# Recurrent-memory attention: output projection of the last tokens for four blocks at once, and a PSUM bank of its own for the memory's softmax sums

One core of a Trainium2 chip runs the kernel. The metric is device time in microseconds (us). Before the change it took 2135.5 us (median of 4 runs from 2131.47 to 2164.58).

## The reference, cut to what matters

```python
def _A_ref(x, mem0, Wq, Wk, Wv, Wo, seg_len):   # x: 1 x 2048 x 512, 32 heads of 128, seg_len 32, mem: 8 x 512
    mem = mem0
    for s in range(n_seg):                       # 64 segments, one after another
        h = concatenate([mem, xs])               # 8 memory rows + 32 tokens
        q, k, v = ...                            # h times Wq, Wk, Wv
        p = softmax(where(mask, q k^T * scale, -1e9))
        o = einsum('bhte,hed->btd', p v, Wo)
        mem = o[:, :M]                           # the next segment needs these 8 rows
        outs.append(o[:, M:])
x = x + A(layernorm(x));  x = x + B(layernorm(x))     # B is a gMLP block
x = x + A(layernorm(x));  x = x + B(layernorm(x))
```

Only the 8 memory rows of o must go around the loop. The last 8 tokens of a segment (rows 24 to 31) are handled separately: the kernel collects their attention outputs in a tile `oB` and multiplies them by Wo later. This deferred product is called "y pass" here. A block is 128 tokens, that is four segments; j4 is a segment's place in its block.

## The kernel before

The end of a segment. `fill()` issues a piece of independent TensorE work. psO takes four PSUM banks, and columns 320 to 383 of each hold sums of the memory rows:

```python
psO = attO.tile([P, 4, 512], F32, name="psO")
psD = att.tile([P, 2, 512], F32, name="psD")
for r in range(2):
    for g in range(2):
        o = psO[:, 2 * r + g, 320:384]
        sums(r, g, o, o, 0, 8, True)       # ones (64 rows) times E: the memory rows' softmax sums
pv(0)                                       # products of the first half of the heads, into psO
...                                         # sums of the tokens, into psD
pv(1)                                       # second half, into psO
Rm = segp.tile([P, 4, 64], F32, name="Rm")
inverse(Rm[:], psO[:, :, 320:384])          # 1/sum as Exp(-Ln(sum)), ScalarE
Rt = segp.tile([P, 2, 512], F32, name="Rt")
inverse(Rt[:], psD[:])
nc.vector.tensor_tensor(out=hview(uT_cur, 0, 4, 0, 8), in0=oview(0, 4, 0, 8), in1=Rm[:]..., op=ALU.mult)
fill(); fill(); run(copies); tok_out(0)
pw = acc.tile([P, 512], F32, name="pw")
wo_pass(pw, uT_cur)                         # memory rows times Wo: the recurrence
build_hA(s + 1, pw)                         # masked copy and transpose: the next segment's input
store_o(s, pw)
fill(); fill(); run(copies); tok_out(1); run(turns)
spare()                                     # layer norm of later blocks, y_add
```

The y pass of one block, in the fills of j4 = 0 of the next one, and the end of the A block:

```python
def wo_pass(po, lhs, heads=range(H)):
    for h in heads:
        n = ...
        for cg in range(4):                 # four quarter-array matmuls of 128 columns
            nc.tensor.matmul(po[32 * cg:32 * cg + 32, 0:128], lhsT=lhs[:, n, :], rhs=wo_rhs(h, cg), ...,
                             tile_position=(0, 32 * cg))
def y_pass(tb):
    pwB = acc.tile([P, DM], F32, name="pwB")
    for h0 in range(0, H, 8):
        wo_pass(pwB, blk_state[tb]["oB"], range(h0, h0 + 8))
        if h0 + 8 < H: yield
    ...                                     # ScalarE copies pwB, 64 KB go to oB_d in memory
def y_load(tb): ...                         # x, oA_d (tokens 0-23) and oB_d (24-31) into xs_y and ot_y, one buffer each
def y_add(tb): ...                          # ot_y + xs_y, store to xd, statistics for the next layer norm

# after the 64 segments:
for _ in y_pass(NB - 1): pass
for tb in (NB - 2, NB - 1):                 # only two blocks are left
    y_load(tb); y_add(tb)
```

The softmax here doesn't subtract the row's maximum and nothing guards it: scores larger than these inputs give would overflow.

## Time and profile before

The two A blocks are recurrences, so I split the profiled execution at the starts of the matmul group pw, the product that gives the next memory, and at the last aggregate of layer-norm statistics, which releases the B block. "Last pw" is that of the 64th segment; one more pw, for the tokens of that segment, follows it and counts as part of the end. All values are us.

| part of the profiled run | before |
|---|---|
| start to first pw of A1 | 88.0 |
| A1, first to last pw (63 intervals) | 789.8 |
| A1, last pw to last aggregate | 20.0 |
| B1, to the first pw of A2 | 247.6 |
| A2, first to last pw | 784.7 |
| A2, last pw to last aggregate | 20.8 |
| B2 to the end | 177.4 |
| span | 2128.3 |

In the list of waits of the whole run (engine, tile and line, then the releaser; us in total, times, longest) the kernel before has

```profile
ACT Rm L619 <- PE psO L614: 211.4, 128, 2.4
DVE uT L671 <- ACT Rm L620: 178.1, 128, 2.7
```

Such totals say who waits for whom and not what that costs: ScalarE's 211 us are mostly time in which it has nothing else to do. What counts is the wait that reaches TensorE, in the group of pw (count | busy us, mean ns | idle us before it and the main releaser):

```profile
L488 PE MATMUL pw<-Wo_sb,uT 128*32 128x128 bf16 x16640 | 267.6, 220 | 81.8 <-DVE uT L671 61.5
```

### The profile page before, as it was taken

To read this page: it belongs to the slowest core of one execution; us is meant where nothing else is said; L and a number is where in the kernel's file an instruction comes from. 1 tells how busy PE (TensorE), PEld (TensorE's weight loads), DVE (VectorE), ACT (ScalarE), POOL (GpSimd) and SP (SyncE) were. 2 spreads that over 40 slices of the span, in tenths; PEclk is the share of its full clock that TensorE was granted. 3 is DMA by queue.
4 is the path that set the end of the run, shared out by engine and by line. 5 is a ranking of instruction groups with operands and counts; after the bars stand their busy time and mean duration, and the time that the engine had idled before them with its cause. 6 is when DMAs were issued, how large, how long until landed. Compare 5 with 4: busy or idle time off the path is not lost.

```text
span 2128.3 us, 104406 instructions
## 1 busy us (share of the span) xinstructions
PE 1811.6 (85%) x48640; PEld 1108.3 (52%) x48640; DVE 1211.8 (57%) x2577; ACT 1031.6 (48%) x1828; POOL 138.8 (7%) x287
## 2 busy tenths in 40 slices
PE   0599999999998999583987999999999999986899
PEld 0355555555555555442754555555555555554476
DVE  1566666666666666440334666666666666664322
ACT  0455555555555555370004555655555555554500
POOL 2000000000000000001230000000000000000022
PEclk9999999999999999895998999999999999997999
DMA  9201111111111110327651011111111111104253
GB/s 382 88 25 35 37 35 35 35 36 38 41 38 35 38 43 27 120 62 267 154 164 61 26 35 35 35 43 36 38 37 46 38 38 37 31 25 155 50 139 90
DMA packets 178675, 145.33 MB, mean 68 GB/s; under 512 B 97472, under 2 KB 148288, under 8 KB 175168
## 3 DMA queue, kind: packets, MB, share of 16 engines
q1 hardware_dynamic: 152544, 83.76, 14.4%
q10 hardware_dynamic: 21728, 30.78, 4.1%
q0 software_dynamic: 3968, 24.12, 3.1%
q8 instruction: 380, 6.23, 1.2%
q14 instruction: 55, 0.45, 0.1%
HBM read 88.13 MB, written 33.70 MB: 57 GB/s over the span
## 4 chain that ended last, share of the span: by engine, by line
PE 65%; ACT 14%; DVE 8%; issue 6%; DMA 6%; POOL 0%; SPq 0%; ACTq 0%; POOLq 0%; DVEq 0%
PE psm L397 21%; PE pw L488 9%; PE pg L216 8%; PE psv L397 6%; PE psb L397 5%; DVE KA L565 4%; PE psO L614 4%; ACT rows L561 4%; PE psS L585 3%; ACT Rm L620 3%; DMA wspT<-in_B_w_sp_dram 2%; ACT Rm L619 2%; DVE uT L671 2%; PE psO L604 2%; PE pwB L488 2%
## 5 line engine op out<-in xcount | busy, mean ns | idle before, releaser
L397 PEld LDWEIGHTS <-hA 128*32 128x32 bf16 x12288 | 305.9, 96 | 300.4 <-DVE hA L537 33.5
L561 ACT CAST rows<-psm 128x512 bf16<-128x512 f32 x512 | 299.7, 585 | 176.6 <-PE psm L397 176.6
L488 PE MATMUL pw<-Wo_sb,uT 128*32 128x128 bf16 x16640 | 267.6, 220 | 81.8 <-DVE uT L671 61.5
L488 PEld LDWEIGHTS <-uT 128*32 128x32 bf16 x16640 | 238.1, 97 | 139.6 <-DVE uT L671 112.2
L397 PE MATMUL psm<-Wq_sb,hA 128*32 128x512 bf16 x4096 | 277.0, 380 | 15.3 <-issue 9.3
L397 PE MATMUL psm<-Wk_sb,hA 128*32 128x512 bf16 x4096 | 271.8, 379 | 0.0
L397 PE MATMUL psv<-Wv_sb,hA 128*32 128x512 bf16 x4096 | 268.0, 382 | 0.0
L630 DVE TENSOR_TENSOR uT<-psO,Rt 128x384 bf16<-128x384 f32 x256 | 137.9, 539 | 201.9 <-ACT Rt L620 201.9
L565 DVE STREAM_TRANSPOSE QQ<-rows 128x512 bf16<-128x512 bf16 x256 | 181.9, 711 | 82.0 <-ACT rows L561 81.8
L216 PE MATMUL pg<-wspT,z2n 128*128 128x256 bf16 (+1 forms) x1536 | 177.0, 277 | 55.1 <-DMA wspT<-in_B_w_sp_dram 55.1
L565 DVE STREAM_TRANSPOSE KA<-rows 128x512 bf16<-128x512 bf16 x256 | 181.8, 710 | 38.2 <-ACT rows L561 35.7
L216 PEld LDWEIGHTS <-z2n 128*128 128x128 bf16 (+1 forms) x1536 | 151.3, 100 | 80.6 <-issue 62.6
L590 ACT ACTIVATE E<-psS 128x448 bf16<-128x448 f32 x256 | 140.0, 547 | 107.5 <-PE psS L585 107.5
L571 DVE CAST VA<-psv 128x512 bf16<-128x512 f32 x256 | 175.4, 685 | 2.4
L397 PEld LDWEIGHTS <-hB 128*32 128x32 bf16 x3072 | 78.3, 97 | 159.9 <-DVE hB L446 71.5
L219 DVE TENSOR_TENSOR gb<-pg,bsp_bc 128x256 f32<-128x256 f32 x96 | 40.6, 423 | 207.5 <-PE pg L216 207.5
L671 DVE TENSOR_TENSOR uT<-psO,Rm 128x256 bf16<-128x256 f32 x128 | 54.3, 424 | 178.1 <-ACT Rm L620 178.1
L619 ACT ACTIVATE Rm<-psO 128x256 f32<-128x256 f32 x128 | 49.0, 383 | 211.4 <-PE psO L614 211.4
L397 PE MATMUL psb<-Wq_sb,hB 128*32 128x512 bf16 x1024 | 70.0, 395 | 91.0 <-DVE hB L446 71.5
L530 POOL COPY QQ<-QTB 128x256 bf16<-128x256 bf16 x128 | 49.4, 401 | 1496.0 <-DVE QTB L476 960.3
L585 PEld LDWEIGHTS <-KA 128*64 128x64 bf16 x2048 | 79.8, 113 | 127.8 <-DVE KA L565 126.5
L620 ACT ACTIVATE Rt<-Rt 128x1024 f32<-128x1024 f32 x128 | 135.4, 1058 | 4.1
(93 smaller groups left out, 2525.3 us busy)
## 6 DMA issues: line engine op xcount, KB each, us to landing
xs<-xd SPq DMA_DIRECT2D x48, 256.0 KB
xs<-xd ACTq DMA_DIRECT2D x48, 256.0 KB
oA_d<-o_sb SPq DMA_DIRECT2D x130, 64.0 KB
xs_y<-xd SPq DMA_DIRECT2D x32, 256.0 KB
xd<-ot_y SPq DMA_DIRECT2D x32, 256.0 KB
Wq_sb<-in_A_Wq_dram POOLq DMA_DIRECT2D x6, 1024.0 KB, 16.0
Wk_sb<-in_A_Wk_dram POOLq DMA_DIRECT2D x6, 1024.0 KB, 24.3
Wv_sb<-in_A_Wv_dram POOLq DMA_DIRECT2D x6, 1024.0 KB, 20.5
```

Source lines behind the costliest of these rows:

```text
L216: nc.tensor.matmul(pg[0:fsz, :], lhsT=z2n[:, st_i, f0:f0 + fsz], rhs=wspT[:, st_i, :], start=(st_i == 0), stop=(st_i == NT - 1))
L397: nc.tensor.matmul(ps[32 * cg:32 * cg + 32, :], lhsT=lhs(kt, cg), rhs=rhs(kt, cg), start=(kt == 0), stop=(kt == KT - 1), tile_position=(0, ...
L488: nc.tensor.matmul(po[32 * cg:32 * cg + 32, 0:128], lhsT=lhs[:, n, :], rhs=wo_rhs(h, cg), start=(h == 0), stop=(h == H - 1), tile_position ...
L561: nc.scalar.copy(r[:], ps[:])
L565: nc.vector.transpose(out=QQ[:, j % 2, :, 0:32] if j < 2 else KA[:, j % 2], in_=r[:])
L571: nc.vector.tensor_copy(VA[:, r].rearrange("p i e -> p (i e)"), ps)
L585: nc.tensor.matmul(pS[64 * g:64 * g + 64, i, c0:80 if K is KA else 112], lhsT=K[:, r, n:n + 2, :].rearrange("p h k -> p (h k)"), rhs=q if ...
L590: nc.scalar.activation(out=E[r][:], in_=pS, func=ACT.Exp, scale=scale)
L619: nc.scalar.activation(out=o, in_=in_, func=ACT.Ln)
L620: nc.scalar.activation(out=o, in_=o, func=ACT.Exp, scale=-1.0)
L630: nc.vector.tensor_tensor(out=hview(uT_nxt, 2 * r, 2 * r + 2, 8, 32), in0=oview(2 * r, 2 * r + 2, 8, 32), in1=Rr[:, :, :, 0:24], op=ALU.mult)
L671: nc.vector.tensor_tensor(out=hview(uT_cur, 0, 4, 0, 8), in0=oview(0, 4, 0, 8), in1=Rm[:].rearrange("p b (n q) -> p b n q", q=8), op=ALU.mult)
```

## The change

Its intent: the memory's sums get a bank of their own, so their reciprocal can start while TensorE still fills psO; and the y pass of 16 segments (512 tokens, 128 deferred rows) runs once, on the whole array. Core of the diff:

```diff
+    onesG = cp.tile([P, 2, P], BF16, name="onesG")       # full-array ones, half of the rows zero
-            for r in range(2):
-                for g in range(2):
-                    o = psO[:, 2 * r + g, 320:384]
-                    sums(r, g, o, o, 0, 8, True)
+            psM = acc.tile([P, 512], F32, name="psM")
+            for g in range(2):
+                o = psM[:, 128 * g:128 * g + 128]
+                nc.tensor.matmul(o, lhsT=onesG[:, g, :], rhs=a_part(0, P, 0, 2, 0, 8), start=(g == 0), ...)
+                nc.tensor.matmul(o, lhsT=onesG[:, g, :], rhs=b_part(0, P, 0, 2, 0, 8), start=False, ...)
...
-            inverse(Rm[:], psO[:, :, 320:384])
+            inverse(Rm[:].rearrange("p g r c -> p (g r c)"), psM[:, 0:256])
...                                                        # uT in two multiplies, one per half
+            spare()                                       # moved here, ahead of the fills
             fill(); fill()
...
-            spare()
...
+        def wo_last(G, heads, pwB):                       # one 128x512 matmul a head
+            for h in heads: ...
+                nc.tensor.matmul(pwB[:], lhsT=oBs[G][:, n, :], rhs=Wo_sb[:, h, :]..., ...)
+        def y_part(G, q): ...                             # 8 heads in j4 = 0 of the q-th block of the next group;
+                                                          # VectorE adds the four partial results in yB
...
-                more = y_pass(tb - 1) if tb > 0 else iter(())
+                more = y_part(tb // 4 - 1, tb % 4) if tb > 3 else iter(())
...
-        for _ in y_pass(NB - 1): pass
-        for tb in (NB - 2, NB - 1):
+        for _ in wo_last(NB // 4 - 1, range(H), pwB): pass
+        for tb in due + list(range(NB - 4, NB)):          # 11, then 12 to 15; block 10 is in flight
             y_load(tb); y_add(tb)
...
-    ident_f = cp.tile(...); maskf = cp.tile(...)          # constants needed only to build others
+    ident_f = tmp.tile(...); maskf = tmp.tile(...)        # pool is closed after the constants: memory used again
-        vsp = ctx.enter_context(tc.tile_pool(name="a_vs", bufs=3))
+        vsp = ctx.enter_context(tc.tile_pool(name="a_vs", bufs=2))
```

The last two pieces make room for the larger `oB`.

More of the change, by code (lines that the diff above doesn't have):

```diff
@@ L53, in _consts @@
     cp = ctx.enter_context(tc.tile_pool(name="consts", bufs=1))
+    tctx = ExitStack()
+    tmp = tctx.enter_context(tc.tile_pool(name="consts_tmp", bufs=1))
     c = {}
-    ident_f = cp.tile([P, P], F32, name="ident_f")
+    ident_f = tmp.tile([P, P], F32, name="ident_f")
     nc.gpsimd.memset(ident_f[:], 0.0)
@@ L62, in _consts @@
     nc.vector.memset(eps_t[:], LN_EPS)
-    maskf = cp.tile([P, 4, 112], F32, name="maskf")
+    maskf = tmp.tile([P, 4, 112], F32, name="maskf")
     nc.gpsimd.memset(maskf[:], 0.0)
@@ L86, in _consts @@
     nc.vector.memset(ones[:], 1.0)
+    onesG = cp.tile([P, 2, P], BF16, name="onesG")
+    nc.vector.memset(onesG[:], 0.0)
+    for g in range(2):
+        nc.vector.memset(onesG[64 * g:64 * g + 64, g, :], 1.0)
     maskM = cp.tile([P, P], mybir.dt.uint16, name="maskM")
@@ L91, in _consts @@
     c["maskM"] = maskM
-    c.update(ident_f=ident_f, ident_bf=ident_bf, eps_t=eps_t, maskN=maskN, ones=ones)
     c["MV"] = [cp.tile([P, 16, 2], F32, name=f"MV{i}") for i in range(2)]
+    tctx.close()
+    c.update(ident_bf=ident_bf, eps_t=eps_t, maskN=maskN, ones=ones, onesG=onesG)
     return c
@@ L275 @@
     c["oA_d"] = dram.tile([S // SEG + 1, P, P], F32, name="oA_d")
-    c["oB_d"] = dram.tile([S // P, P, P], F32, name="oB_d")
+    c["oB_d"] = dram.tile([S // 512, P, DM], F32, name="oB_d")
     nblocks = opts["nblocks"]
@@ L356, in a_block @@
     scale = float(DH) ** -0.5
-    maskN, ones = c["maskN"], c["ones"]
+    maskN, ones, onesG = c["maskN"], c["ones"], c["onesG"]
     with ExitStack() as ctx:
@@ L450, in ln_turn @@
             blk_state[tb].update(hB=hB, KTB=KTB, QTB=QTB, VB=VB)
-        copies, turns = [], []
+        copies, turns, adds = [], [], []
         def run(todo):
@@ L489, in wo_pass, with y_part @@
                                      start=(h == 0), stop=(h == H - 1), tile_position=(0, 32 * cg))
-        def y_pass(tb):
+        yB = {}
+        def wo_last(G, heads, pwB):
+            for h in heads:
+                n = h // 8 * 8 + 2 * (h % 4) + h // 4 % 2
+                nc.tensor.matmul(pwB[:], lhsT=oBs[G][:, n, :], rhs=Wo_sb[:, h, :].rearrange("p (kt g el) -> p g kt el", kt=4, g=4),
+                                 start=(h == heads[0]), stop=(h == heads[-1]))
+                if h % 2 == 1:
+                    yield
+        def y_part(G, q):
             pwB = acc.tile([P, DM], F32, name="pwB")
-            for h0 in range(0, H, 8):
-                wo_pass(pwB, blk_state[tb]["oB"], range(h0, h0 + 8))
-                if h0 + 8 < H:
+            for k, _ in enumerate(wo_last(G, range(8 * q, 8 * q + 8), pwB)):
+                if k < 3:
                     yield
             def out():
-                oB_sb = wk.tile([P, P], F32, name="oB_sb")
-                nc.scalar.copy(oB_sb[:], pwB[:, 0:128])
-                nc.sync.dma_start(oB_d[tb], oB_sb[:])
-            copies.append(out)
+                if q == 0:
+                    yB[G] = wk.tile([P, DM], F32, name="yB", bufs=1)
+                    nc.vector.tensor_copy(yB[G][:], pwB[:])
+                else:
+                    nc.vector.tensor_tensor(out=yB[G][:], in0=pwB[:], in1=yB[G][:], op=ALU.add)
+                if q == 3:
+                    nc.sync.dma_start(oB_d[G], yB.pop(G)[:])
+            adds.append(out)
             yield
@@ L513, in y_load @@
                 nc.sync.dma_start(ot[32 * j + 24:32 * j + 32, :, :],
-                                  oB_d[tb].rearrange("(cg r) c -> r cg c", cg=4)[8 * j:8 * j + 8])
+                                  oB_d[tb // 4, 32 * (tb % 4) + 8 * j:32 * (tb % 4) + 8 * j + 8, :].rearrange("r (cg c) -> r cg c", cg=4))
             xo = ot[:].rearrange("p cg c -> p (cg c)")
@@ L524, in a_block @@
         seg_state = {}
+        oBs = {}
         def prep_segment(s):
@@ L551, in segment @@
             uT_cur, uT_nxt = uT[s % 2], uT[(s + 1) % 2]
-            if j4 == 0:
-                blk_state[tb]["oB"] = blkp.tile([P, H, 32], BF16, name="oB")
-            oB = blk_state[tb]["oB"]
-            E = [None] * 2
+            if s % 16 == 0:
+                oBs[tb // 4] = blkp.tile([P, H, P], BF16, name="oB")
+            oB = oBs[tb // 4]
+            E = segp.tile([P, 2, 4, 112], BF16, name="E")
             def qk(j):
@@ L588, in scores, with a_part, b_part @@
                                              start=(i == 0 and K is KA), stop=True, tile_position=(0, 64 * g), skip_group_check=True)
-                E[r] = segp.tile([P, 4, 112], BF16, name="E")
-                nc.scalar.activation(out=E[r][:], in_=pS, func=ACT.Exp, scale=scale)
+                nc.scalar.activation(out=E[:, r], in_=pS, func=ACT.Exp, scale=scale)
             def close(r):
-                nc.vector.tensor_tensor(out=E[r][:], in0=E[r][:], in1=maskN[:, j4, :].unsqueeze(1).to_broadcast([P, 4, 112]), op=ALU.mult)
-            def b_part(r, g, lo, hi):
-                return E[r][64 * g:64 * g + 64, :, 80:112].rearrange("p i (s q) -> p i s q", s=2)[:, :, :, lo:hi]
-            def a_part(r, g, lo, hi):
-                return E[r][64 * g:64 * g + 64, :, 0:80].rearrange("p i (s q) -> p i s q", s=2)[:, :, :, lo:hi]
-            def sums(r, g, o, oB, lo, hi, first):
-                w = ones[64 * g:64 * g + 64, :]
-                nc.tensor.matmul(o, lhsT=w, rhs=a_part(r, g, lo, hi), start=first, stop=True, skip_group_check=True)
-                nc.tensor.matmul(oB, lhsT=w, rhs=b_part(r, g, 0 if lo == 0 else 8, 8 if lo == 0 else 16),
-                                 start=False, stop=True, skip_group_check=True)
+                nc.vector.tensor_tensor(out=E[:, r], in0=E[:, r], in1=maskN[:, j4, :].unsqueeze(1).to_broadcast([P, 4, 112]), op=ALU.mult)
+            def a_part(p0, p1, r0, r1, lo, hi):
+                e = E[p0:p1, r0:r1].rearrange("p r i c -> p (r i) c")[:, :, 0:80]
+                return e.rearrange("p n (s q) -> p n s q", s=2)[:, :, :, lo:hi]
+            def b_part(p0, p1, r0, r1, lo, hi):
+                e = E[p0:p1, r0:r1].rearrange("p r i c -> p (r i) c")[:, :, 80:112]
+                return e.rearrange("p n (s q) -> p n s q", s=2)[:, :, :, lo:hi]
             def pv(r):
@@ L614, in pv @@
                             nc.tensor.matmul(o if V is VA else ends(o), lhsT=V[64 * g:64 * g + 64, r, i, :],
-                                             rhs=E[r][64 * g:64 * g + 64, i, c0:c1].rearrange("p (s q) -> p s q", s=2),
-                                             start=False, stop=True, skip_group_check=True)
+                                             rhs=E[64 * g:64 * g + 64, r, i, c0:c1].rearrange("p (s q) -> p s q", s=2),
+                                             start=(i == 0 and V is VA), stop=True, skip_group_check=True)
             def inverse(o, in_):
@@ L631, in tok_out @@
                                         in1=Rr[:, :, :, 0:24], op=ALU.mult)
-                nc.vector.tensor_tensor(out=hview(oB, 2 * r, 2 * r + 2, 8 * j4, 8 * j4 + 8), in0=oview(2 * r, 2 * r + 2, 32, 40),
+                nc.vector.tensor_tensor(out=hview(oB, 2 * r, 2 * r + 2, 8 * (s % 16), 8 * (s % 16) + 8), in0=oview(2 * r, 2 * r + 2, 32, 40),
                                         in1=Rr[:, :, :, 24:32], op=ALU.mult)
@@ L653, in segment @@
             v_out(1, v1[:])
+            psM = acc.tile([P, 512], F32, name="psM")
+            for g in range(2):
+                o = psM[:, 128 * g:128 * g + 128]
+                nc.tensor.matmul(o, lhsT=onesG[:, g, :], rhs=a_part(0, P, 0, 2, 0, 8), start=(g == 0), stop=True, skip_group_check=True)
+                nc.tensor.matmul(o, lhsT=onesG[:, g, :], rhs=b_part(0, P, 0, 2, 0, 8), start=False, stop=True, skip_group_check=True)
             psO = attO.tile([P, 4, 512], F32, name="psO")
             psD = att.tile([P, 2, 512], F32, name="psD")
-            for r in range(2):
-                for g in range(2):
-                    o = psO[:, 2 * r + g, 320:384]
-                    sums(r, g, o, o, 0, 8, True)
@@ L661, in segment @@
-            pv(0)
-            for r in range(2):
-                for g in range(2):
-                    o = psD[:, g, 256 * r:256 * r + 256]
-                    sums(r, g, o, o.rearrange("p (n q) -> p n q", q=32)[:, :, 24:32], 8, 40, r == 0)
-            pv(1)
-            Rm = segp.tile([P, 4, 64], F32, name="Rm")
-            inverse(Rm[:], psO[:, :, 320:384])
-            Rt = segp.tile([P, 2, 512], F32, name="Rt")
-            inverse(Rt[:], psD[:])
-            nc.vector.tensor_tensor(out=hview(uT_cur, 0, 4, 0, 8), in0=oview(0, 4, 0, 8),
-                                    in1=Rm[:].rearrange("p b (n q) -> p b n q", q=8), op=ALU.mult)
+            pv(0)
@@ new lines, in segment @@
+            for part, q0, q1, c0 in ((a_part, 8, 40, 0), (b_part, 8, 16, 24)):
+                for r in range(2):
+                    for g in range(2):
+                        o = psD[:, g, 256 * r:256 * r + 256].rearrange("p (n q) -> p n q", q=32)[:, :, c0:32]
+                        nc.tensor.matmul(o, lhsT=ones[64 * g:64 * g + 64, :], rhs=part(64 * g, 64 * g + 64, r, r + 1, q0, q1),
+                                         start=(part is a_part and r == 0), stop=True, skip_group_check=True)
@@ new lines, in segment @@
+            pv(1)
+            Rm = segp.tile([P, 2, 2, 64], F32, name="Rm", bufs=1)
+            inverse(Rm[:].rearrange("p g r c -> p (g r c)"), psM[:, 0:256])
+            Rt = segp.tile([P, 2, 512], F32, name="Rt", bufs=1)
+            inverse(Rt[:], psD[:])
+            for r in range(2):
+                nc.vector.tensor_tensor(out=hview(uT_cur, 2 * r, 2 * r + 2, 0, 8), in0=oview(2 * r, 2 * r + 2, 0, 8),
+                                        in1=Rm[:, :, r].rearrange("p g (n q) -> p g n q", q=8), op=ALU.mult)
@@ L684, in segment @@
             run(copies)
+            run(adds)
             tok_out(1)
             run(turns)
-            spare()
             if s + 1 < NSEG:
@@ L700, in a_block @@
         prep_segment(0)
+        due, ys = [], []
         for s in range(NSEG):
@@ L703, in a_block @@
             if j4 == 0:
-                if tb > 1:
-                    y_load(tb - 2)
-                more = y_pass(tb - 1) if tb > 0 else iter(())
+                more = y_part(tb // 4 - 1, tb % 4) if tb > 3 else iter(())
             if j4 == 1:
@@ L712, in spare @@
             def spare():
+                if ys:
+                    y_add(ys.pop(0))
+                if tb % 4 == 3 and j4 == 1 and tb > 4:
+                    due.extend(range(tb - 7, tb - 3))
+                if due:
+                    ys.append(due.pop(0))
+                    y_load(ys[0])
                 if j4 == 0 and tb + 1 < NB:
                     ln_turn(tb + 1)
-                if j4 == 0 and tb > 1:
-                    y_add(tb - 2)
                 if j4 == 3 and tb + 2 < NB:
@@ L723, in a_block @@
         store_o(NSEG, pw)
-        for _ in y_pass(NB - 1):
-            pass
-        run(copies)
-        for tb in (NB - 2, NB - 1):
+        pwB = acc.tile([P, DM], F32, name="pwB")
+        for _ in wo_last(NB // 4 - 1, range(H), pwB):
+            pass
+        yl = wk.tile([P, DM], F32, name="yB", bufs=1)
+        nc.scalar.copy(yl[:], pwB[:])
+        nc.sync.dma_start(oB_d[NB // 4 - 1], yl[:])
+        for tb in ys:
+            y_add(tb)
+        for tb in due + list(range(NB - 4, NB)):
             y_load(tb)
```

## The prediction

> **What bounds the kernel now.** I read the page first, then all waits, then the timeline of some segments (a segment is 32 tokens; each of the two A blocks runs 64 of them in sequence), then the chain of the end of an A block. The page:
>
> ```profile
> PE   1811.6 (85%) x48640; PEld 1108.3 (52%) x48640; DVE 1211.8 (57%) x2577; ACT 1031.6 (48%) x1828; POOL 138.8 (7%) x287
> ...
> PE 65%; ACT 14%; DVE 8%; issue 6%; DMA 6%; POOL 0%; SPq 0%; ACTq 0%; POOLq 0%; DVEq 0%
> ```
>
> TensorE is the busiest, yet a third of the chain is not TensorE: the recurrence hops PE, ACT, DVE and back. The timeline of one ordinary segment shows the hop that the change is about:
>
> ```profile
> 511.23 0.39 DVE L593 TENSOR_TENSOR E<-E,maskN 128x448 bf16<-128x448 bf16 x1 [0.25 <-ACT E L590]
> ...
> 512.62 0.18 PE L614 MATMUL psO<-E,VB 64*128 64x32 bf16 x2
> 512.73 0.55 PEld L397 LDWEIGHTS <-hB 128*32 128x32 bf16 x16
> 512.73 1.05 PE L397 MATMUL psb<-Wq_sb,hB 128*32 128x512 bf16 x16
> 512.84 0.38 ACT L619 ACTIVATE Rm<-psO 128x256 f32<-128x256 f32 x1 [1.65 <-PE psO L614]
> 513.26 0.42 ACT L620 ACTIVATE Rm<-Rm 128x256 f32<-128x256 f32 x1
> 513.58 1.01 ACT L619 ACTIVATE Rt<-psD 128x1024 f32<-128x1024 f32 x1
> 513.71 0.42 DVE L671 TENSOR_TENSOR uT<-psO,Rm 128x256 bf16<-128x256 f32 x1 [1.37 <-ACT Rm L620]
> 514.18 1.79 PEld L488 LDWEIGHTS <-uT 128*32 128x32 bf16 x128 [0.90 <-DVE uT L671]
> 514.18 1.97 PE L488 MATMUL pw<-Wo_sb,uT 128*32 128x128 bf16 x128 [0.41 <-DVE uT L671]
> ```
>
> Rm reads the memory's sums, complete at about 511.9, but starts only after the last product of the second half (512.62 + 0.18), because both sit in the banks of psO. So Ln, Exp and the multiply (512.84 to 514.13) run in the open; the filler psb hides 0.87 of it and PE stands idle 0.41. After pw, masked copy and transpose lead to the next psm at 517.06. With no filler, pw-to-pw is 11.97 us as well (852.34 to 864.31), so the ordinary segment is bound by this chain, and filler is free. From the 128 starts of pw: in all intervals but those around j4 = 0 (the first segment of a block of 128 tokens) 11.97 is the floor. Above 63 x 11.97 = 754 the first A block has 35.7 us, the second 30.6; 25.5 and 26.8 of it lie behind the pw of j4 = 0. There the old y pass sits:
>
> ```profile
> 437.65 1.35 PE L488 MATMUL pw<-Wo_sb,uT 128*32 128x128 bf16 x83 [0.51 <-issue]
> ...
> 441.67 0.46 PE L488 MATMUL pwB<-Wo_sb,oB 128*32 128x128 bf16 x19 [2.05 <-issue]
> ```
>
> 256 tiny matmuls and as many weight loads in a row, then PE stops with nothing to wait for; then psm waits for the copy out of pwB.
>
> The end of an A block is a chain of transfers: block 15 is loaded, added, its statistics taken, and only then can the B block start (rstd needs all 16).
>
> ```profile
> 891.15 2.15 DMA oB_d<-oB_sb
> 893.32 0.27 SPq L513
> ...
> 894.31 1.65 DMA ot_y<-oB_d
> ```
>
> The first and last of these are from the chain of waits, the middle one the queue's issue; in the timeline what follows is:
>
> ```profile
> 896.14 0.69 DVE L520 TENSOR_TENSOR ot_y<-ot_y,xs_y 128x512 f32<-128x512 f32 x1 [13.89 <-DMA ot_y<-oB_d]
> 896.86 0.34 SPq L521 DMA_DIRECT2D xd<-ot_y  x1
> ```
>
> **What the Trainium skill says.** "PSUM — Partial Sum Buffer", section on bank collisions: two engines must be kept apart by bank and 32-partition quadrant, not by address. The trace agrees: Rm waits for matmuls that write other columns of its banks. "TensorE: Matmul & The Clock Gate", Back-to-back issue gap: N/2.4 + 2.5 ns, 216 for 512 columns; here groups of 16 psm matmuls, each on a quarter of the array and four at once, follow one another at 0.87 us (505.95, 506.82, 507.69), 4 x 217 ns, so it agrees. "Runtime: NRT & Kernel Launch", Instruction fetch mechanics: instructions are streamed in 16 KiB blocks of 256. The page's instruction queue has 380 packets and 6.23 MB, 16.4 KB each, and the stops in pw and pwB fall at fixed places in the stream; that they are fetch is my reading, not shown. "DMA: Bandwidth & Descriptors", Anatomy: about 2 us fixed per transfer, mostly the receipt; the 64 KB store above took 2.15, so it agrees.
>
> **The change, part by part.** (1) Sums. Eight matmuls of 64 columns become four of 128 on the full array. They need both halves of E, ready at 511.62. I put four times 56 ns from there plus one switch of array shape, 0.09 (the gap seen between the end of one stream and the next shape), so the first product starts at 511.97 instead of 511.73. The psD sums take 0.27; the second half then starts at 512.49 rather than 512.38, where it waited for VA anyway: 0.11 lost. psM is complete at 512.03; Rm's Ln and Exp run 512.08 to 512.92, uT follows in two pieces of about 0.28 (128x128 pieces of oB take 0.277) to 513.44. Rt follows Rm on ACT and ends at 514.99 instead of 515.68, so the token products that stand ahead of the masked copy on DVE end at 515.69. On PE: last product issued 512.73, filler from 512.84 to 513.71, pw from 513.76 (32 groups of four at 55.6 ns stream in 1.78; with the 0.19 until the last result is in PSUM, 515.73), masked copy 515.78, transpose and psm 0.68 later as before (516.38 to 517.06): 516.46. The second filler ends at the same moment (515.60 + 0.87). Saved: 0.60 with DVE and PE nearly tied, I take 0.58. Without filler the Rt path decides: 0.69.
>
> (2) y. 2048 quarter-array matmuls per A block (16 x 128) become 128 of 512 columns; PE drops from 48640 to 48640 - 4096 - 512 + 256 = 44288 matmuls. Of the time in it only the excess around j4 = 0 counts. What comes in its place: in 12 segments per A block, two times four matmuls of 216. The second four end 516.7 in the frame above, then DVE adds 128x512 f32 (0.69, as in xo) before psm may take that bank: psm at 517.44, so +0.38 each over 11.97, 4.6 per A block. Some fetch stops stay; I keep 6.
>
> (3) y_add, ln_turn and ln_apply move into the gap of DVE between uT and Rt (1.5 us); y_add is 0.65 + 0.69 + 0.18. Nearly free.
>
> Per A block: 45 segments with filler x 0.58 = 26.1; 7 without x 0.69 = 4.8; excess 35.7 (30.6) less 10.6 = 25.1 (20.0). Sum 56 and 51, 107. Ten chained hops never all come as sums say; I take 100.
>
> (4) The end. Before, two blocks are left for after the last segment, and the first is prefetched. After, 10 is in flight, 11 to 15 are left, and xs_y and ot_y have one buffer each, so load, add and store run one after another. A round: eight issues 0.335 apart and 1.65 landing = 4.0, wait 0.2, add 0.7, store about 2.3 (0.34 to issue and the fixed part; stores here made the next load wait up to 2.9) = 7.2. Block 11 goes beside the last Wo pass: 32 x 0.216 = 6.9 us in place of 2.3 plus its stops of 1.2 to 4. Then 12, 13 and 14 are three rounds in the open (21.6), the larger copy and store cost about 0.5, and the rest of the 11 round and slower pass about 4: +26 per A block, +52.
>
> Sum: 2135.6 - 100 + 52 = 2087.6.
>
> **Rivals.** (a) The end costs more: the queue might keep program order, so that block 10's store waits for yB's; one more round each, +15: 2103. Against: the queue already runs out of program order (block 14's load comes before block 15's oB store). Or early loads of the next block's weights slow the stores: one xd store took 8.27 us at 1934.30. (b) The psM switch costs several tenths, or uT's first piece waits for the whole of psO: then PE and DVE, nearly tied, lose 0.2 to 0.3 per segment, 128 x 0.25 = 32: 2120. (c) The stops behind pwB were all due to the flood of small instructions and vanish, and the chain gains all it can: 2075; with a tail that hides two rounds, 2060. (d) Fetch stops move to pw, which alone still sends 256 instructions in 1.8 us and now has less idle ahead of it: half of the 45 us I count for excess comes back: 2110.
>
> **Range and chances.** The gain in the loop is 100 +- 13, the loss at the end 52 +- 12, independent: 48 +- 18, so 2088, 8 in 10 between 2064 and 2112. The 2% mark below 2135.6 is 2092.9, slightly above my middle; the two fast runs before (2131 and 2136) put it at 2091. Faster 0.56, same 0.41, slower 0.03.
>
> **What would show it.** Rm starts before the second half of the products ends, and PE's wait for uT before pw (61.5 us in all) falls below 10. Ordinary pw-to-pw intervals: 11.4. Intervals behind j4 = 0: 12.3 with a y part. PE's stops without a cause inside pwB are gone. From the last pw to the last aggregate of statistics: 20.0 and 20.8 us before, 46 after. ACT copies of pwB vanish; DVE gains 24 adds or copies of 0.69. The prediction is wrong if the ordinary interval stays above 11.7 (step 1), if the end grows by under 15 or over 40 us (step 4), or if the time moves elsewhere, as into the B blocks.

## The result

The kernel after took 2103.01 us (median of 4 runs, 2101.05 to 2104.00; before 2135.51 in the same rounds). The ratio is 0.9858, with a 95% interval of 0.984 to 0.9877: 1.4% faster, which lies within 2%. Ratios here are the mean time of one kernel's runs over that of the other's runs of the same rounds, so not quite the ratio of the medians. Executions over 1.5% slower than the fastest of the same kernel are left out of the means.

| part of the profiled run | before | after | difference | predicted |
|---|---|---|---|---|
| start to first pw of A1 | 88.0 | 92.2 | +4.3 | 0 |
| A1 loop | 789.8 | 736.4 | -53.4 | -56 computed |
| A1 end | 20.0 | 54.2 | +34.2 | +26 |
| B1 to first pw of A2 | 247.6 | 250.8 | +3.2 | 0 |
| A2 loop | 784.7 | 734.8 | -50.0 | -51 computed |
| A2 end | 20.8 | 55.0 | +34.1 | +26 |
| B2 to the end | 177.4 | 178.9 | +1.6 | 0 |
| span | 2128.3 | 2102.3 | -26.0 | -48, with 100 taken for the 107 |

The profiled run before was one of the faster ones, so the profiles differ by 26.0 and the medians by 32.5.

The loop did what was predicted; starts and ends cost more. From the page of the kernel after:

```profile
PE   1788.5 (85%) x44288; PEld 1076.1 (51%) x44288; DVE 1247.1 (59%) x2732; ACT 1024.3 (49%) x1798; POOL 138.6 (7%) x287
...
PE 66%; ACT 11%; DVE 9%; issue 7%; DMA 4%; SPq 1%; POOL 1%; ACTq 0%; DVEq 0%; POOLq 0%
```

4352 matmuls are gone, yet TensorE's busy time hardly moved (1811.6 to 1788.5), because four quarter-array matmuls ran side by side. ScalarE's share of the chain fell from 14% to 11%. The waits and the group that answer to those of before:

```profile
ACT Rm L636 <- PE psM L676: 117.6, 128, 1.1
```

```profile
L495 PE MATMUL pw<-Wo_sb,uT 128*32 128x128 bf16 x16640 | 266.6, 219 | 30.5 <-issue 23.4
```

uT is no longer what pw waits for: of the 30.5 us left, 23.4 are stops without a visible cause. The timeline of a segment that has a y part (columns: start, length, engine, line, operation, tiles; idle before and releaser in brackets):

```profile
512.11 0.22 PE L676 MATMUL psM<-E,onesG 128*128 128x128 bf16 x1
...
512.37 0.38 ACT L636 ACTIVATE Rm<-psM 128x256 f32<-128x256 f32 x1 [0.92 <-PE psM L676]
...
512.52 0.44 PE L684 MATMUL psD<-E,ones 64*128 64x256 bf16 x8
...
512.78 0.42 ACT L637 ACTIVATE Rm<-Rm 128x256 f32<-128x256 f32 x1
...
513.12 1.04 PE L504 MATMUL pwB<-Wo_sb,oB 128*128 128x512 bf16 x4
...
514.09 1.97 PE L495 MATMUL pw<-Wo_sb,uT 128*32 128x128 bf16 x128
...
515.99 1.04 PE L504 MATMUL pwB<-Wo_sb,oB 128*128 128x512 bf16 x4
...
516.96 1.05 PE L404 MATMUL psm<-Wq_sb,hA 128*32 128x512 bf16 x16
517.07 0.69 DVE L521 TENSOR_TENSOR yB<-pwB,yB 128x512 f32<-128x512 f32 x1 [0.32 <-PE pwB L504]
```

Rm starts 0.04 us after psM and is done at 513.20; uT follows from it before the filler pwB ends, so pw starts without a wait. The last two lines matter as well: psm, the next segment's first product, starts before VectorE reads pwB. The prediction had psm wait for that read.

What bounds such an interval now? The stretch from one pw to the next in an undisturbed segment, before and after (us, then the same columns as in the table by stretches further down):

```profile
412.36:424.33 11.97, 11.44 (x336) 6.54 (x336) 8.27 (x17) 7.42 (x14) 1.14 (x3) 1.00 0.03 9
337.69:349.05 11.36, 11.19 (x337) 6.64 (x332) 8.42 (x18) 7.42 (x14) 0.00 (x0) 1.00 0.04 10
```

Before, TensorE stood idle for 0.41 us of it, waiting for uT. After, it is busy for 11.19 of 11.36 us, so TensorE's own work sets the interval, and there is little slack left in which a stop could hide.

The end of A1, the matmuls, the queue SPq's issues and the statistics picked from the timeline:

```profile
829.47 0.32 SPq L543 DMA_DIRECT2D xd<-ot_y  x1
...
833.82 2.44 PE L495 MATMUL pw<-Wo_sb,uT 128*32 128x128 bf16 x128 [3.19 <-issue]
836.22 0.32 SPq L533 DMA_DIRECT2D ot_y<-oA_d  x1
...
837.84 0.29 PE L495 MATMUL pw<-Wo_sb,uT 128*32 128x128 bf16 x3 [1.57 <-issue]
838.06 8.99 PE L504 MATMUL pwB<-Wo_sb,oB 128*128 128x512 bf16 x32
...
842.39 0.33 SPq L543 DMA_DIRECT2D xd<-ot_y  x1
...
843.12 0.18 DVE L114 BATCH_NORM_AGGREGATE MV<-bnst 128x2 f32<-128x6 f32 x1
...
847.70 0.32 SPq L755 DMA_DIRECT2D oB_d<-yB  x1
848.07 0.42 SPq L530 DMA_DIRECT2D xs_y<-xd  x1
...
882.72 0.18 DVE L114 BATCH_NORM_AGGREGATE MV<-bnst 128x2 f32<-128x6 f32 x1
```

Block 9's store (829.47) is issued while the B block already fetches eight early tiles of x, 256 KB each; the DMA engines are 97% busy from 828 to 834. So block 10's loads into ot_y start only at 836.22. Its store goes out at 842.39, but block 11's loads start at 848.07, right behind the store of yB, for which the queue waits 5.0 us. In the queue, then, block 10's store stands ahead of yB's store and block 11's loads behind it, in A2 as in A1, and yB waits for the Wo pass. (The program text has yB's store first, so this is not simply program order. Block 10's delay is not on the chain that ended last: it is done before yB is ready.) The aggregates then come at 854.48, 861.30, 868.36, 875.66 and 882.72, so a round takes 7.1 us. Behind the Wo pass stand five rounds, 11 to 15; before, it was block 15's alone, and the prediction had four, with block 11's beside the pass.

The 34.2 us of A1 are therefore 5.7 from the last pw to the store of the last Wo pass's result (19.0 against 13.4), 0.3 in the first round behind it, and 28.2 for four more rounds. In A2 they are 5.2, 0.9 and 28.0.

The Trainium skill, "DMA: Bandwidth & Descriptors", section "Issuing engines are not separate DMA queues", says that DMAs of all issuing engines run on the same 16 engines and interleave. The trace agrees: in the rounds of the end the next load into ot_y goes out 2.1 us after a store of ot_y (853.74 to 855.83); here it went out 6.75 us after it (829.47 to 836.22).

The pass itself takes 8.99 us and not 32 x 0.216 = 6.9. The table by stretches (us, busy time of each engine, granted clock, DMA share, GB/s) of the kernel after shows why:

```profile
core 0: us, PE busy (x) PEld busy (x) DVE busy (x) ACT busy (x) POOL busy (x), PEclk, DMA share, GB/s
...
838.00:842.00 4.00, 4.00 (x13) 1.46 (x11) 0.33 (x1) 0.27 (x1) 0.00 (x0) 0.50 0.41 92
842.00:847.00 5.00, 5.00 (x24) 2.08 (x22) 1.24 (x3) 0.00 (x0) 0.00 (x0) 1.00 0.92 322
```

TensorE had stood still for 3.19 and 1.57 us before the pass, and its clock was granted at 0.50 for the pass's first 4 us. The Trainium skill, "TensorE: Matmul & The Clock Gate", section "What's actually happening", has this: half rate after an idle window of about 3.4 us, full rate again after about 3.4 us of work. The trace agrees in size, not to the tenth: half rate began at about 835.1, although the stop of 3.19 us was shorter than that window and TensorE was working again, and full rate came back at 842.0, 3.9 us into the pass; in A2, 4.5 us into it (878.5 to 883.0).

### The profile page after: what moved, and what is told of

It reads as the page before. It is cut to its first block, busy times and chain, and to the rows that moved or that the text cites. A ratio compares the mean times of both kernels' runs of the same rounds, so it can differ in the third digit from the quotient of the medians.

```text
span 2102.3 us, 95923 instructions
## 1 busy us (share of the span) xinstructions
PE 1788.5 (85%) x44288; PEld 1076.1 (51%) x44288; DVE 1247.1 (59%) x2732; ACT 1024.3 (49%) x1798; POOL 138.6 (7%) x287
## 4 chain that ended last, share of the span: by engine, by line
PE 66%; ACT 11%; DVE 9%; issue 7%; DMA 4%; SPq 1%; POOL 1%; ACTq 0%; DVEq 0%; POOLq 0%
PE psm L404 22%; PE pw L495 11%; PE psb L404 9%; PE pg L223 8%; DVE KA L588 4%; ACT rows L584 4%; ACT E L612 3%; PE psO L631 3%; PE pwB L504 3%; PE psS L608 3%; DVE E L615 2%; DMA xb<-in_A_x_dram 2%; PE psM L675 2%; PE psD L684 2%; PE py L234 1%
## 5 line engine op out<-in xcount | busy, mean ns | idle before, releaser
L404 PEld LDWEIGHTS <-hA 128*32 128x32 bf16 x12288 | 304.4, 96 | 309.1 <-DVE hA L560 54.2
L495 PE MATMUL pw<-Wo_sb,uT 128*32 128x128 bf16 x16640 | 266.6, 219 | 30.5 <-issue 23.4
L404 PE MATMUL psm<-Wq_sb,hA 128*32 128x512 bf16 x4096 | 272.5, 381 | 11.7 <-DVE hA L560 11.6
L495 PEld LDWEIGHTS <-uT 128*32 128x32 bf16 x16640 | 245.2, 97 | 70.4 <-issue 31.9
L636 ACT ACTIVATE Rt<-psD 128x1024 f32<-128x1024 f32 x128 | 128.6, 1005 | 0.1
```

Of the source, the lines that this page charges most:

```text
L404: nc.tensor.matmul(ps[32 * cg:32 * cg + 32, :], lhsT=lhs(kt, cg), rhs=rhs(kt, cg), start=(kt == 0), stop=(kt == KT - 1), tile_position=(0, ...
L636: nc.scalar.activation(out=o, in_=in_, func=ACT.Ln)
```

## The experiments

Seven kernels ran, all with correct results. The parts of their profiled runs, in us, beside the two kernels of the change:

| kernel | start | A1 loop | A1 end | B1 to A2 | A2 loop | A2 end | rest | median, timed |
|---|---|---|---|---|---|---|---|---|
| before | 88.0 | 789.8 | 20.0 | 247.6 | 784.7 | 20.8 | 177.4 | 2135.5 |
| after | 92.2 | 736.4 | 54.2 | 250.8 | 734.8 | 55.0 | 178.9 | 2103.0 |
| s1_sums_only | 88.5 | 779.6 | 19.9 | 254.0 | 770.2 | 19.9 | 176.6 | 2097.9 |
| y1_y_only | 94.2 | 766.1 | 53.0 | 253.7 | 764.5 | 52.2 | 178.1 | 2159.1 |
| c1_starts | 88.1 | 736.6 | 53.9 | 246.0 | 737.3 | 54.7 | 178.1 | 2096.1 |
| t1_tail | 91.9 | 736.8 | 37.3 | 259.0 | 738.9 | 40.2 | 183.9 | 2091.0 |
| sp1_spare_late | 91.5 | 742.7 | 56.0 | 252.6 | 740.6 | 55.4 | 176.7 | 2118.3 |
| f1_dummy | 93.7 | 740.5 | 53.7 | 248.6 | 741.9 | 54.1 | 178.4 | 2112.4 (1 run) |
| b1_best | 88.3 | 740.4 | 24.0 | 247.6 | 743.0 | 24.9 | 179.4 | 2049.3 |

The first batch (s1, y1, c1, t1) had its own runs of the kernel before, median 2137.4; the second (sp1, f1, b1) 2136.9.

### s1_sums_only: the sums without the rest

```diff
 (the kernel before, with)
+    onesG, psM, E in one tile, Rm from psM, uT in two multiplies   # as in the change
 (old y pass, old place of spare(), old end)
```

> The kernel before with the memory's sums in a bank of their own (E one tile, uT in two pieces); the y pass, the place of y_add and the end as before. Theory (the bank and the y pass each give about half of the 103 us that the loops lost): 2085 us, ordinary pw-to-pw interval near 11.45 instead of 11.97, the ends of the A blocks 20 and 21 us as before, so faster than the changed kernel. Rival (the loop is bound by TensorE's instruction supply, and all the gain is the y pass): 2120 or more, intervals 11.8 or more.

Measured: 2097.85 us (2092.13 to 2110.43), ratio 0.9823 (0.9787 to 0.9859). That is no slower than the whole change (the intervals of 0.9823 and 0.9858 overlap), since nothing is lost at the ends. The profile fell on the slowest run, at a mean clock of 0.943 where its other runs (2092 to 2099 us) had 0.970 to 0.973, so its loop times are not taken for a size; what they do show is where nothing was won. In A2, the 16 intervals behind j4 = 0, with the old y pass in 15 of them, sum to 218.5 us; before they summed to 218.4. The low clock does not explain that: the last nine, from 1485 us on, where the clock was granted at 1.00, sum to 123.6 against 124.3. The timeline of such a segment:

```profile
434.97 0.67 PE L492 MATMUL pw<-Wo_sb,uT 128*32 128x128 bf16 x33
436.31 1.53 PE L492 MATMUL pw<-Wo_sb,uT 128*32 128x128 bf16 x95 [0.67 <-issue]
437.62 0.67 PE L492 MATMUL pwB<-Wo_sb,oB 128*32 128x128 bf16 x33
440.05 0.63 PE L492 MATMUL pwB<-Wo_sb,oB 128*32 128x128 bf16 x31 [1.76 <-issue]
```

The chain is shorter, but TensorE stops for 0.67 and 1.76 us; in each loop its stops without a visible cause add up to 38.7 us, against 27.1 and 23.2 before. So the sums pay only where there is no flood of small matmuls, and the two halves of the change help each other.

### y1_y_only: the new y pass with the old sums

```diff
 (the kernel after, with)
-            psM = acc.tile(...)             # and its four matmuls
+            sums into columns 320:384 of psO, Rm from psO, uT in one multiply   # as before
```

> The changed kernel with the old sums (eight matmuls into psO, Rm after the last product, uT in one piece). Theory: loops 50 to 55 us shorter than before, ends 68 us and starts 9 us longer: 2155 to 2160, slower than before. Rival (the y pass is the gain): 2120 or less.

Measured: 2159.07 us (2155.33 to 2163.55), ratio 1.0102 (1.0081 to 1.0123), as expected: slower than before (1.0%, clear of noise, though within 2%). The loops fell by 23.7 and 20.2 us, almost the 25.1 and 20.0 that the prediction had for the excess behind j4 = 0. The floor stayed at 11.97 us. From here to the kernel after, the loops lose a further 29.7 us each, for which the prediction had 26.1 + 4.8 = 30.9: this is what the sums are worth once the small matmuls are gone. About 22 of it lie in the 47 intervals not behind j4 = 0, and 8.0 and 6.9 in the others, where the prediction had no gain.

### A bank alone, with the old narrow matmuls

The change also went from eight matmuls on 64 rows to four on the full array. A version of s1 that kept the narrow ones and only moved them to psM was built and refused by a race check before it could run: two tiles of different rows of the array would write one bank with nothing to order them. So the bank and the wider matmuls are tested only together; the traces show the bank's part, that Rm no longer waits for psO.

### c1_starts: the start and the memory's first load

```diff
-    tctx.close()                            # in the constants: frees ident_f and maskf
+    c["tctx"] = tctx                        # closed after the loads of x instead
+        if "m0" not in c:                   # mem0 and its permuted copy only for the first A block
             m0 = rowp.tile(...); ...
```

> The changed kernel with the temporary constants held until the first loads of x are through, and mem0 fetched for the first A block only. Theory: the first pw of the first A block comes back from 92.2 to about 88 us, the start of the second A block loses 4.5: 2094. Rival (these shifts are noise of the transfers at the start): 2103 within 2.

Measured: 2096.11 us (2095.31 to 2099.78), ratio 0.9811 (0.9792 to 0.983); the first pw is back at 88.1 and B1 to A2 takes 246.0. So 7 of the lost microseconds came from memory that is shared over time. In the kernel after, the first tile of x takes the place of the temporary mask and waits until GpSimd has built it and VectorE has copied it out (first load 9.55, first cast 46.28; before, the first cast was at 6.32), and the large weight loads go ahead of it. In A2, mem0's tile lies where the B block still stores its result:

```profile
SPq L416 <- DMA xd<-xo: 13.5, 1, 13.5
```

VectorE's copy of mem0 waits 13.84 us for it (to 1110.16) and stands ahead of the layer norm in program order, so the A block starts later. The first pw is clear; of the second part the size is less so, since B1 to A2 takes 248.6 to 253.7 us in the other kernels with that load (t1 apart) and 246.0 and 247.6 in the two without.

### t1_tail: the end's loads with more buffers

```diff
-        for tb in due + list(range(NB - 4, NB)):
-            y_load(tb); y_add(tb)
+        Rl = segp.tile([P, 2, 512], F32, name="Rt", bufs=1)      # free after the last segment: two buffers
+        half = [Rl[:, k]... for k in range(2)]
+        y_load(NB - 5, half[0], "xs"); y_add(NB - 5)
+        y_load(NB - 4, half[1]); y_load(NB - 3, None, "xs"); y_add(NB - 4)   # one load ahead of the add
+        ...
```

> The changed kernel; in the last five blocks of y each load has a buffer that its predecessor does not hold (half of Rt twice, and the free xs), one load ahead of the add. Theory (one buffer chains load, add and store): the rounds shrink from 7.0 us to the 3.5 that the queue needs to issue nine loads and a store, the ends from 54 to 40 us, 2075. Rival (the store's receipt or the traffic sets the round whatever the buffers): rounds stay above 6, 2098 or more.

Measured: 2091.04 us (2088.9 to 2094.93), ratio 0.9785 (0.9767 to 0.9803). The rounds shrank as expected, from 7.1 to 3.3 to 4.2 us, and the ends to 37.3 and 40.2 (-17 and -15). But only 12 of those 32 us arrived. A wait that was not there before ate most of the rest. In t1's list of waits just after the end of A1 stands:

```profile
PE pz2a L168 <- DMA w_in_sb<-in_B_w_in_dram: 6.5, 1, 6.5
```

The B block's weights w_in lie over Rt. As Rt now was a load buffer to the end, their load went out at 867.13, after the last aggregate; in the kernel after it went out at 840.52, well ahead of the end. B1 to A2 grew by 8 us and the last part by 5 (where the same wait is 5.5). The A2 loop was 4 longer, for no cause that was looked for. The wait at the end had hidden a load, and taking it away showed the load.

### sp1_spare_late: y_add and the layer norm back at the end of the segment

```diff
             nc.vector.tensor_tensor(out=hview(uT_cur, ...))
-            spare()
             fill(); fill()
...
             run(turns)
+            spare()
```

> The kernel after, but with y_add, ln_turn and ln_apply back at the end of a segment, as in the kernel before. Theory (the move is nearly free, since VectorE idles 1.13 us there too, until the first row copy): 2103 to 2107, loops 735 to 739 us. Rival (the move is a good part of the gain, because y_add's 1.5 us held up the next transposes): 2115 or more, with intervals of 12 us and more where a y_add stands.

Measured: 2118.28 us (2117.02 to 2123.13), ratio 0.9919 (0.9903 to 0.9934). Against the kernel after (0.9858) that is 0.6% or 13 us; the loops grew by 6.3 and 5.8. My theory was wrong and the rival right. VectorE of this run, around one y_add:

```profile
447.31 0.58 ACT L584 CAST rows<-psm 128x512 bf16<-128x512 f32 x1 [0.34 <-PE psm L404]
...
447.93 0.65 DVE L542 TENSOR_TENSOR ot_y<-ot_y,xs_y 128x512 f32<-128x512 f32 x1
...
448.61 0.70 DVE L113 BATCH_NORM_STATS2 bnst<-ot_y 128x6 f32<-128x512 f32 x1
...
449.34 0.18 DVE L114 BATCH_NORM_AGGREGATE MV<-bnst 128x2 f32<-128x6 f32 x1
449.44 0.68 DVE L588 STREAM_TRANSPOSE QQ<-rows 128x512 bf16<-128x512 bf16 x1
```

The row copy is done at 447.89 and its transpose starts at 449.44, 1.55 us late. Four transposes of 0.7 follow one another at 0.6, while new rows come every 0.87, so about 0.8 of the 1.55 is made up. The idle time that I had counted on, 1.13 us, was shorter than the work.

### f1_dummy: the same TensorE work with many or few instructions

```diff
 (the kernel after; in j4 = 0 of blocks 0 to 3, whose fills are empty)
+    more = dummy(small=(tb % 2 == 0))
+    # small: 32 heads x 4 matmuls of 128x128 columns on quarter arrays, 128 weight loads (1.8 us)
+    # else:  8 matmuls of 128x512 (1.73 us); the result is copied and not used
```

> The kernel after with a useless Wo pass as filler of the first segment of blocks 0 to 3, whose fillers are empty: in blocks 0 and 2 the old form (128 matmuls on quarter arrays with 128 weight loads, 1.8 us of TensorE), in blocks 1 and 3 eight matmuls of 512 columns (1.73 us). If the stops behind the old pass come from the number of small instructions (supply), the intervals after j4 = 0 in blocks 0 and 2 grow to 12.5 to 14 us with stops inside pwD or pw that wait for nothing, and those of blocks 1 and 3 stay at 11.5 to 11.8, though TensorE has the same work. If it is the work or the bank that matters, both kinds grow alike or neither does.

Measured (one look, 2112.4 us). The intervals behind j4 = 0 in blocks 0 to 3 were 13.06, 11.53, 13.29 and 11.53 us in A1, and 12.96, 11.52, 13.75 and 11.94 in A2: against the same intervals of the kernel after, every block with the small form lost 1.0 to 2.2 us, and those with the large form at most 0.4. The small form in block 2:

```profile
188.01 1.07 PE L534 MATMUL pwD<-Wo_sb 128*32 128x128 bf16 x64
188.92 1.67 PE L495 MATMUL pw<-Wo_sb,uT 128*32 128x128 bf16 x105
192.00 0.52 PE L495 MATMUL pw<-Wo_sb,uT 128*32 128x128 bf16 x23 [1.41 <-issue]
```

And the large form in block 1:

```profile
141.27 1.04 PE L538 MATMUL pwD<-Wo_sb 128*128 128x512 bf16 x4
142.23 1.97 PE L495 MATMUL pw<-Wo_sb,uT 128*32 128x128 bf16 x128
144.14 1.04 PE L538 MATMUL pwD<-Wo_sb 128*128 128x512 bf16 x4
```

TensorE's work is the same; the number of instructions is 256 against 16. The two forms also differ in how much of the array a matmul takes, so by itself this shows only that the stops follow the small form. The DMA view of a tenth of a microsecond (189.40 to 189.50) in the first case holds one packet of the instruction queue:

```profile
q8 instruction: 1, 0.02, 62.6%
```

TensorE goes on at 192.00, 2.6 us after it. I looked for the last such packet ahead of four more stops: before, at 439.2 for the stop that ends at 441.67, and at 887.4 for 889.67; after, at 835.4 for 837.84; here, at 94.5 for 97.40. The lag is 2.3 to 2.9 us each time. It holds for nearly all: of the stops of 0.4 us or more without a visible cause ahead of pw, pwB, psb or psm, 54 of 55 before and 21 of 22 after end 2.2 to 3.0 us after the start of the last such packet, where a moment taken at random between 100 and 820 us does so in 17 to 18% of cases (counted in the packed traces). That a stop is the wait for this packet's instructions is inferred from these findings together; no record names it.

### b1_best: both starts and ends mended

```diff
 (c1_starts, with)
+        def y_late(q): ...        # last group: 96 columns (blocks 12 to 14), 12 heads each in the fills of segments 61 to 63;
+                                  # its rows go from yB to the blocks' tiles directly
-        for _ in wo_last(NB // 4 - 1, range(H), pwB): pass
+        wo_pass(pwB, oBs[NG][:, :, 96:128])      # block 15 alone, old form
+        # blocks 8 to 11 two at a time, 12 to 14 loaded ahead, into dead KTB, QTB, VB and oB tiles;
+        # none of these lies where the B block's w_in goes
```

> The starts as in c1_starts, and an end as short as that of the kernel before: the last Wo pass of blocks 12 to 14 (96 columns) runs as filler of segments 61 to 63, only block 15's old pass on quarter arrays is left for after the loop; blocks 8 to 14 are loaded into buffers that are dead by then. Theory (the end costs +34 us per A block only because five blocks are added one after another behind a late Wo pass): from the last pw to the last aggregate of statistics 20 to 25 us instead of 54, so about 2 x 32 us less than c1_starts' 2096: 2028 to 2042. Rival (as in t1_tail, a load of the B block then waits for one of the borrowed buffers or the queue is too full, so the time reappears in B's start): 2055 or more, with a wait of several us on a load right after the last aggregate.

Measured: 2049.31 us (2041.58 to 2053.04), ratio 0.9585 (0.9565 to 0.9606), faster than both kernels and than s1. The ends are 24.0 and 24.9, as the theory said. It misses the expected 2042 by 7 us. The loops account for most: 740.4 and 743.0 against c1's 736.6 and 737.3, because the last three intervals, with the heavier fills, take 12.1 to 13.1 us. The end of A1 in this run:

```profile
837.69 1.50 PE L499 MATMUL pwB<-Wo_sb,oB 128*32 128x128 bf16 x93
840.97 0.68 PE L499 MATMUL pwB<-Wo_sb,oB 128*32 128x128 bf16 x35 [1.77 <-issue]
...
846.42 0.40 SPq L836 DMA_DIRECT2D oBl_d<-oB_sb  x1
...
852.58 0.18 DVE L114 BATCH_NORM_AGGREGATE MV<-bnst 128x2 f32<-128x6 f32 x1
```

Something is left here: the copy of block 15's rows is ready at 841.96, but its store goes out at 846.42, behind twelve small transfers of the other blocks in the same queue.

## Why the prediction was right, and where it was not

The predicted 2088 was 15 us too low, inside the range of 2064 to 2112. The outcome of 1.4% faster fell in "within 2%", to which it gave 0.41 against 0.56 for faster. In the profiles the predicted gain of 48 became 26.0, and the table shows where the 22 went: 16.3 at the two ends, 7.5 at the two starts, 1.6 in the rest; the loops gave 3.4 more than the 100 taken.

- **(1) Sums: mechanism right, total right partly by luck.** Rm starts before the second half of the products, and 29.7 us a loop lie between y1 and after, predicted 30.9. The groups of psM follow at 0.06 us, and from the start of the last one to the first product are 0.15, which leaves about the 0.09 for the switch of shape that the prediction had. But 11.36 us is the floor of the ordinary intervals and not, as predicted with 11.4, what most of them take. Of the 47 per loop that are not behind j4 = 0, only 13 and 15 lie within 0.05 of it; their medians are 11.71 and 11.63, at the very limit of 11.7 beyond which the prediction called itself wrong. Before, 29 and 38 lay that near 11.97. Against 11.39 these intervals cost 16 and 13 us a loop, where 6 had been kept for stops; the next point's error has about the same size and the other sign.
- **(2) y pass: right in its size, wrong in one term.** y1 gives 23.7 and 20.2 for the 25.1 and 20.0. But psm does not wait for the read of pwB: the intervals behind j4 = 0 with a y part are 11.18 to 11.88 us and not 12.3. Here the sums pay too: 12 intervals at about 0.8 us less than predicted are some 10 us a loop, in the careful direction. That they offset the long intervals of (1) is luck, and it is why 103.4 arrived where 100 was taken.
- **The two do not add when taken from the kernel before.** s1 alone lost its gain in the segments of the old y pass. The prediction took both limits of those segments away together and did not count each for itself.
- **(3) The move of y_add: right that it costs nothing at its new place.** It is worth 13 us against the old place, which the prediction did not say.
- **(4) The end: mechanism right, size off.** The term that failed is "Block 11 goes beside the last Wo pass": 34 us each instead of 26. Block 11's loads stood in the queue behind yB's store, which waits for the pass, so that there is one round of 7.1 us more in the open: four more than before (28.2 us) where the prediction had three (21.6). The rest, 6.0 us against about 4.5, is TensorE's stops ahead of the pass and the halved clock, for which 6.9 us of pass became 8.99. The rounds themselves (7.1 against 7.2) were right. Rival (a) named one more round and 2103, the number that came, but not for the reason it gave: block 10's store did not wait for yB's, block 11's loads did; and the early loads of the next block (of x rather than weights) delayed block 10 without being on the chain. That its number is met to the microsecond is chance.
- **What the prediction left out:** the starts, +4.3 and +3.2. It took the smaller constants and pools for bookkeeping. c1 shows that they cost 7 us.
- **Rival (d)**, that the stops move to pw, which has less idle ahead of it, came in part. In the loop of A1, waits of pw without a visible cause, in y1 and in the kernel after:

```profile
PE pw L495 <- issue: 1.6, 6, 0.4
PE pw L495 <- issue: 6.8, 15, 1.0
```

In A2 they are 0.5 and 6.1 us. All in all the ordinary intervals lie 32 us above their floor in both loops together, against 14 before and 20 in y1. That is some 12 to 18 us, and (d) had half of 45. The loops' total hid it.

What stays open: the few microseconds by which the B1 part differs between kernels that do not touch it (246.0 to 254.0 apart from t1). In s1, 3.9 of its 6.4 are a longer wait for the transposed loads of w_sp (50.4 against 46.5), whose cause I did not look for.

## What to carry to other kernels

Batching deferred work cheapens the loop but leaves a longer queue at its end: count the rounds after the last iteration, one by one, in the order of the queue that carries them, with the transfers of the next stage already running; here the end's 68 us took two thirds of what the loop had gained. Where a chain is cut below TensorE's own work, stops that its waits had covered can come into the open (at pw 2.1 us in the loops of y1, 12.9 after). A version that keeps most of the loop's gain and spreads the last batch over the last iterations reached 2049. When buffers shrink or are reused to make room, ask for every reuse which later load now waits for which earlier reader.

## What the Trainium skill lacked or had wrong

- "Runtime: NRT & Kernel Launch", Instruction fetch mechanics, calls the cost of crossing a block of 256 instructions "mostly hidden", because dispatch, at about 20 cycles an instruction, is slower than the fill. In these runs 256 small TensorE instructions as filler, next to pw's own 256, cost 1.0 to 2.2 us a segment that 16 large ones did not (12.96 to 13.75 against 11.52 to 11.94), and TensorE resumed 2.3 to 2.9 us after an instruction packet. That these stops are the fetch is inferred. The page has no number for how densely instructions may come before it shows.
- "TensorEngine Tiling (Array Packing)", Key Properties, says that a change of tiling mode drains TensorE, with no number. Here the first 64-row product started 0.15 us after the last full-array psM matmul had started (512.11 to 512.26), where psM matmuls follow one another at 0.06, so the switch took about 0.09 us.
- "DMA: Bandwidth & Descriptors", Anatomy, gives about 2 us fixed, for the path of the GpSimd; the stores here go by a hardware queue. A 256 KB store beside 2 MB of other loads (DMA 97% busy) let the next load go after 6.75 us here, and no page has a number for such a store. The same page, "Issuing engines are not separate DMA queues", calls the time to initiate a DMA usually small; in the rounds of the end, eight issues 0.345 us apart are 2.8 of 7.1 us.
